# Joint score tiles, one low-rank add, key copies on ScalarE, and seven-product down projections from batch 1 on

## The chip, the cores and the metric

The kernel runs on one core of one Trainium2 chip. The metric is the device time of one execution in microseconds (us). The engines are named as in the profile: PE is TensorE's matmul, PEld its weight load, DVE VectorE, ACT ScalarE, POOL GpSimd, SP the engine that issues most DMAs. Each engine works through its own instructions in the order of the program and waits for the others by semaphores; an instruction that waits holds up all that stand behind it on its engine.

## The reference: what is computed

Four batches, 8 heads, 768 positions, head dimension 64. Attention with a local window of 96 positions and 8 global keys, with a linear bias by distance and a slope per head, and after it a mixer: a low-rank sum over positions (rank 32) and a feed-forward layer 512 to 2048 to 512.

```python
scores = scale * q @ k.T
rel = pos[:, None] - pos[None, :]
keep = is_global | ((rel >= 0) & (rel < n_local))
dist = where(is_global & ~is_local, n_local, abs(rel))
slopes = 2.0 ** (-8.0 * (arange(H) + 1) / H)
a = softmax(where(keep, scores - slopes * dist, -1e9))
x = concat_heads(a @ v)                # (4, 768, 512)
u = x + ((x.T @ U) @ V).T              # over positions, rank 32
out = u + relu(u @ w_ch1) @ w_ch2
```

With 8 heads the slope of head h+1 is half that of head h.

## The kernel before

**Tiling.** The program order is written out by hand (`manual_schedule`). Attention goes by pairs of heads: pair i is batch i // 4 and heads 2(i % 4) and the next one, 16 pairs. A pair's scores are three chunks of 512, 512 and 384 columns (diagonal blocks of 128 and the blocks beside them, with the 8 global keys copied into the first columns of the key blocks `kA`). A chunk of one head is one PSUM bank of 512 fp32 columns. PSUM's eight banks are the tags `sc` (2), `ob` (1), `cps` (2) and `th` (3).

**Batch 0** (pairs 0 to 3) adds the bias on PE (L352, a matmul with `slI` and `rel16`), and ACT takes the exponential from PSUM chunk by chunk (`st_SE`, L379). Its low-rank sum is made on PE too.

**Batches 1 to 3** add the bias on DVE: `st_S` makes a chunk's scores for both heads (`scores`, L360 and L367), and `s_dve` (L392) does one step for each head, score times scale over slope plus the table `relcat`, into `sp`; `st_E` (L404) takes the exponential of a whole head, 1408 columns. `st_V` multiplies by the values into `ob` (L416, L420), DVE normalises (L425, L439) and POOL makes an fp16 copy (L440). The low-rank sum of a pair is `st_M1` (L449, copied by L453), `st_MT` (L466, copied by L467) and `st_M3` (L503), whose result DVE adds to `x_sb` in two halves (L508), the first from `sc`, the second from `ob`; POOL copies to fp16 (L512), and `st_X` (L492) transposes by DMA into `uT`. The keys of a later pair are transposed by DMA (`turn`) and copied by DVE (`st_K`, L335 and L336).

**Feed-forward** goes by groups of 256 positions: group (b, g), three to a batch. A group has 8 up units (L609: 8 matmuls of 256 columns each; ACT's relu, L614, writes `htr`). Its down part is one of two kinds. Plain (`mk_down`): 8 units of four 512-column matmuls (L639), and two DVE adds (L644). Seven products (`mk_product`, the groups in `WG`): x1 to x4 into the bank `cx` and y1 to y3 into `cy`, each 8 matmuls of 256 columns (L659) and a DVE add of 256 columns into `x_sb` (L664), from sums s1 to s4 of halves of `htr` and t1 to t4 of quarters of the weights (L540). Each s is made in two halves of 512 columns: the first after four up units, the second after eight. A product's first four matmuls read the first half, its last four the second. In most groups the order of products is x1, y1, y2, x2, y3, x3, x4, in the last x1, y1, x2, y2, x3, y3, x4. y2 reads s1, x2 s2, y3 s4, x3 s3.

**The loop** of i = 4 to 17 (L774) sets the order around the change. One iteration does the scores of pair i, the values and low-rank sum of pair i-1, and between these steps `fill` (L691) issues units: 11 an iteration from i = 9 on. `unit` (L697) alternates an up unit of the next group with a down unit of the present one, as long as there are both. The up units of a batch are queued in the middle of i = 9, 13 and 17 (`queue_ff`); what is left after i = 17 is drained at the end. After each unit `fill` issues one queued DVE sum (`jobs`); a product that needs a sum that is not issued yet issues the sums up to it (`need`). Steps of an iteration, with units between them: scores chunk 0, values of the first head, chunk 1, values of the second head, chunk 2, M1, first exponential, MT, key copy of the next pair, M3, second exponential, transpose.

The weight sums t1, t2 and t4 (eight sums of 1024 columns with t3) are queued while the last plain group's down units run: group (2,0), in i = 14 and 15. Their tile takes one of the three `x_sb` buffers.

Of the kernel before, what the change touches and what calls it, by code (L numbers as in the profile page):

```python
# [20 lines left out]
def kernel(  # L21
# [17 lines left out]
    P = 128  # L39
# [28 lines left out]
    WG = ((2, 1), (2, 2), (3, 0), (3, 1), (3, 2))  # L68
# [11 lines left out]
    def ps_sc(tag="sc"):  # L80
        return psum.tile([P, 512], FP32, name="sc", tag=tag, bufs=2)
# [84 lines left out]
    setup = scp.tile([P, 384], I32, name="setup", tag="ep0")  # L166
# [16 lines left out]
    relcat = cst.tile([P, 640], FP32, name="relcat")  # L183
# [17 lines left out]
    for vt in vbuf:  # L201
        nc.gpsimd.memset(vt[:, :, :, D:D + 1], 1.0)
    nc.gpsimd.tensor_copy(relcat[:, 0:512].rearrange("p (a c) -> p a c", a=2), rel3[:, 0:2])
    nc.gpsimd.tensor_copy(relcat[:, 512:640], relB[:, 0:P])
    finish_table(
        relcat, relcat[0:NG, 0:512].rearrange("p (a c) -> p a c", a=2)[:, :, P:]
    )
# [22 lines left out]
    def new_batch(b):  # L230
        xs[b] = xp.tile([P, NSB, DM], FP32, name="x_sb", tag="x_sb", bufs=3)
        x16s[b] = xp.tile([P, NP, NSB, P], FP16, name="x16", tag="x16")
        tmps[b] = xp.tile([P, DM], FP16, name="tmp16", tag="tmp16", bufs=3)
        uTs[b] = xp.tile([P, NDC, S], FP16, name="uT", tag="uT")
# [97 lines left out]
    def st_K(i):  # L332
        kT = kts[i]
        kA = kp.tile([P, NSB - 1, P], FP16, name="kA", tag="kA")
        nc.vector.tensor_copy(kA.rearrange("d n p -> d (n p)"), kT[:, 0:S - P])  # L335
        nc.vector.tensor_copy(  # L336
            kA[:, 1:, 0:NG], kT[:, 0:NG].unsqueeze(1).broadcast_to((P, NSB - 2, NG))
# [5 lines left out]
    def scores(i, c, on_pe):  # L343
# [5 lines left out]
        scs = [ps_sc("cps" if on_pe and (i + c) % 2 else "sc") for hi in range(2)]  # L349
# [21 lines left out]
        return [(sc, c0, tot, r0) for sc in scs]  # L371

    def st_SE(i, c):

        if c == 0:
            for hi in range(2):
                eps[i, hi] = scp.tile([P, W], FP16, name=f"ep{hi}", tag=f"ep{hi}")
        for hi, (sc, c0, tot, _) in enumerate(scores(i, c, True)):
            nc.scalar.activation(  # L379
                eps[i, hi][:, c0:c0 + tot], sc[:, 0:tot], AF.Exp, scale=qk_scale  # L380
            )

    relfs = (relcat[:, 0:512], relcat[:, 256:512].unsqueeze(1).broadcast_to((P, 2, 256)), relcat[:, 256:640])

    def s_dve(i, hi, got):
        sc, c0, tot, r0 = got
        if c0 == 0:
            sps[i, hi] = scp.tile([P, W], FP32, name=f"sp{hi}", tag=f"sp{hi}", bufs=1)
        dst, got = sps[i, hi][:, c0:c0 + tot], sc[:, 0:tot]
        if c0 == 512:  # L390
            dst, got = (t.rearrange("p (a c) -> p a c", a=2) for t in (dst, got))
        nc.vector.scalar_tensor_tensor(  # L392
            out=dst, in0=got,
            scalar=qk_scale / slope[2 * (i % NP) + hi], in1=relfs[c0 // 512],
# [3 lines left out]
    def st_S(i, c):  # L398
        for hi, got in enumerate(scores(i, c, False)):
            s_dve(i, hi, got)  # L400

    def st_E(i, hi):
        ep = scp.tile([P, W], FP16, name=f"ep{hi}", tag=f"ep{hi}")
        nc.scalar.activation(  # L404
            ep, sps.pop((i, hi)), AF.Exp, scale=slope[2 * (i % NP) + hi]
        )
        eps[i, hi] = ep

    def st_V(i, hi):
        b, h = i // NP, 2 * (i % NP) + hi  # L410
        ep, vt, vA = eps.pop((i, hi)), vts[i], vas[i]
# [15 lines left out]
        x16 = x16s[b][:, i % NP, :, hi * D:(hi + 1) * D]  # L427
# [15 lines left out]
    def st_M1(i):  # L443
        b, dc = i // NP, i % NP
        ch = slice(dc * P, (dc + 1) * P)
        if b:
            tps = ps_ob()
            for n in range(NSB):
                nc.tensor.matmul(  # L449
                    tps[:, 0:R], x16s[b][:, dc, n], u16[:, n, 0:R],  # L450
# [5 lines left out]
        for n in range(NSB):  # L456
            nc.tensor.matmul(
                tps[:, 0:P], u16[:, n], x16s[b][:, dc, n],
# [10 lines left out]
    def st_M2(i):  # L469
        b, dc = i // NP, i % NP  # L470
        ch = slice(dc * P, (dc + 1) * P)
        for g in range(2):
# [5 lines left out]
            for t in range(NTG):  # L478
                nc.tensor.matmul(
                    ups[:, t * P:(t + 1) * P], x16s[b][:, dc, NTG * g + t], ident16,  # L480
# [9 lines left out]
    def st_X(i):  # L490
# [3 lines left out]
            x16s[b][:, dc].rearrange("p n d -> p (n d)"),  # L494
        )

    def st_M3(i, g):
        b, dc = i // NP, i % NP
        ch = slice(dc * P, (dc + 1) * P)
        ups = ps_ob() if g else ps_sc()  # L500
        for t in range(NTG):
            n = NTG * g + t
            nc.tensor.matmul(  # L503
                ups[:, t * P:(t + 1) * P], v16w[:, n * P:(n + 1) * P], tmps[b][:, ch],
# [386 lines left out]
```

## Time and profile before

| | us |
|---|---|
| median of 3 runs (lowest, highest) | 233.54 (232.63, 234.28) |
| the profiled execution | 232.94 |
| its span | 231.0 |
| from the span's start to the loop's first bias steps of i = 5 | 40.1 |
| i = 9 to 15, from one iteration's first bias step to the next | 12.04, 12.23, 12.01, 12.02, 12.21, 11.86, 12.30 |
| drain: last product's start | 226.64 |

The granted TensorE clock is 1.00 in every stretch. The page gives shares of busy time over the whole span; since matmuls overlap in the pipeline, a row's length is not what a matmul costs in a stream: that is read from the starts of rows that follow each other. A row of the time line with xN merges N instructions of one line. What the number in brackets after a row says is how long the engine sat idle before it, and which instruction ended that.

Rows of the groups that the change touches (busy us, mean ns of one):

```profile
L392 DVE SCALAR_TENSOR_TENSOR sp<-sc,relcat 128x512 f32<-128x512 f32 x48 | 31.0, 685 | 6.6 <-PE sc L367 5.7 <-ACT ep L404 0.4
...
L392 DVE SCALAR_TENSOR_TENSOR sp<-sc,relcat 128x384 f32<-128x384 f32 x24 | 12.3, 552 | 8.9 <-PE sc L360 8.9
...
L508 DVE TENSOR_TENSOR x_sb<-sc,x_sb 128x384 f32<-128x384 f32 x12 | 6.7, 556 | 3.8 <-PE sc L503 3.7
...
L335 DVE COPY kA<-kT 128x640 f16<-128x640 f16 x8 | 2.5, 319 | 0.2 <-DMA kT<-k 0.2
```

### The profile page before, as it was taken

How to read it: one execution, taken by the hardware profiler on the slowest of the kernel's cores; microseconds unless marked ns; L12 is line 12 of the kernel's file. 1: busy time of each engine (PE TensorE's matmuls, PEld its weight loads, DVE VectorE, ACT ScalarE, POOL GpSimd, SP SyncE). 2: the span in 40 equal slices, each digit the busy share in tenths (PEclk: the TensorE clock that was granted, in tenths of full speed). 3: DMA queues.
4: the chain of work that ended last, by engine and by line, in shares of the span. 5: the costliest groups of instructions: out<-in, count | busy, mean ns of one | idle time of the engine just before them, and what ended most of it. 6: DMA issues, size and time to landing. Idle time of an engine off the chain costs nothing.

```text
span 231.0 us, 5678 instructions
## 1 busy us (share of the span) xinstructions
PE 223.2 (97%) x2324; PEld 161.8 (70%) x2324; DVE 152.7 (66%) x350; ACT 110.9 (48%) x167; POOL 80.5 (35%) x131
## 2 busy tenths in 40 slices
PE   7989999999999999999999999999999999999994
PEld 2455678788644457766666656866688888888883
DVE  3697797868677667566656675779895524444452
ACT  6776957685621313827363707473633334333320
POOL 6399728577444243433424051504120100000000
PEclk9999999999999999999999999999999999999999
DMA  6997998999999999897786955633131302011112
GB/s 183 321 280 201 280 203 188 261 259 175 213 210 244 209 315 216 220 182 188 157 226 134 258 140 145 148 100 79 32 81 48 79 3 91 1 48 45 45 48 91
DMA packets 86561, 36.66 MB, mean 159 GB/s; under 512 B 74152, under 2 KB 83592, under 8 KB 86536
## 3 DMA queue, kind: packets, MB, share of 16 engines
q1 hardware_dynamic: 81480, 32.01, 55.1%
q0 software_dynamic: 5056, 4.29, 12.3%
q8 instruction: 18, 0.29, 0.5%
q14 instruction: 7, 0.06, 0.1%
HBM read 27.46 MB, written 6.29 MB: 146 GB/s over the span
## 4 chain that ended last, share of the span: by engine, by line
PE 86%; POOL 3%; DMA 3%; ACT 3%; DVE 2%; issue 1%; SPq 1%; POOLq 0%
PE hps L609 35%; PE cps L639 22%; PE cx L659 8%; PE cy L659 5%; PE sc L360 4%; DMA vst<-in_v_dram 3%; PE ob L420 2%; PE ob L416 2%; PE sc L367 2%; ACT htr L614 1%; ACT ep L404 1%; PE tp L250 1%; PE sc L503 1%; PE ob L503 1%; SPq L105 1%
## 5 line engine op out<-in xcount | busy, mean ns | idle before, releaser
L614 ACT ACTIVATE htr<-hps 128x512 f16<-128x512 f32 x96 | 56.6, 598 | 85.0 <-PE hps L609 82.2
L609 PE MATMUL hps<-uT,w 128*128 128x256 f16 x756 | 96.2, 273 | 0.5 <-DVE uT L485 0.3
L609 PEld LDWEIGHTS <-w 128*128 128x128 f16 x756 | 70.5, 98 | 11.3 <-issue 0.4
L639 PE MATMUL cps<-w,htr 128*128 128x512 f16 x224 | 56.9, 379 | 0.0
L392 DVE SCALAR_TENSOR_TENSOR sp<-sc,relcat 128x512 f32<-128x512 f32 (+1 forms) x72 | 43.3, 641 | 15.5 <-PE sc L360 8.9
L404 ACT ACTIVATE ep<-sp 128x1408 f16<-128x1408 f32 x24 | 32.8, 1374 | 16.3 <-DVE sp L392 16.3
L512 POOL CAST x<-x_sb 128x768 f16<-128x768 f32 x12 | 10.3, 856 | 60.5 <-DVE x_sb L508 60.5
L639 PEld LDWEIGHTS <-htr 128*128 128x128 f16 x224 | 19.1, 97 | 16.6
L440 POOL CAST x<-x_sb 128x384 f16<-128x384 f32 x30 | 15.8, 525 | 26.8 <-DVE x_sb L439 26.7
L360 PEld LDWEIGHTS <-kT 64*128 64x128 f16 x192 | 8.2, 93 | 15.1 <-issue 13.5
L540 DVE TENSOR_TENSOR s<-htr 128x512 f16<-128x512 f16 x20 | 9.3, 464 | 12.7 <-ACT htr L614 12.7
L439 DVE TENSOR_TENSOR x_sb<-ob,rcp 128x384 f32<-128x384 f32 x30 | 16.7, 558 | 1.0
L659 PEld LDWEIGHTS <-s 128*128 128x128 f16 x160 | 15.5, 98 | 1.8
L360 PE MATMUL sc<-qT,kT 64*128 64x128 f16 x192 | 16.7, 221 | 0.0
L420 PE MATMUL ob<-v,ep 128*128 128x65 f16 x192 | 16.2, 193 | 0.0
L420 PEld LDWEIGHTS <-ep 128*128 128x128 f16 x192 | 13.8, 98 | 2.7 <-ACT ep L379 0.3
L664 DVE TENSOR_TENSOR x_sb<-cx,x_sb 128x256 f32<-128x256 f32 x20 | 8.5, 423 | 10.1 <-PE cx L659 10.0
L136 POOL CAST v<-vst 128x768 f16<-128x768 f32 x16 | 13.4, 839 | 4.5 <-DMA vst<-in_v_dram 4.5
L367 PE MATMUL sc<-qT,kA 64*128 64x128 f16 x160 | 14.1, 216 | 0.9 <-DVE kA L286 0.9
L379 ACT ACTIVATE ep<-sc 128x512 f16<-128x512 f32 (+1 forms) x24 | 12.0, 559 | 5.1 <-PE sc L367 4.8
L416 PE MATMUL ob<-vA,ep 128*128 128x65 f16 x160 | 14.3, 194 | 0.2 <-DVE vA L312 0.2
L659 PEld LDWEIGHTS <-htr 128*128 128x128 f16 x120 | 11.7, 98 | 1.3
(102 smaller groups left out, 269.4 us busy)
## 6 DMA issues: line engine op xcount, KB each, us to landing
qst<-in_q_dram SPq DMA_DIRECT2D x16, 384.0 KB, 4.2
kst<-in_k_dram SPq DMA_DIRECT2D x16, 384.0 KB, 4.9
vst<-in_v_dram SPq DMA_DIRECT2D x16, 384.0 KB, 3.4
out_dram<-x_sb SPq DMA_DIRECT2D x23, 256.0 KB, 2.3
w<-in_moe_w_ch_dram POOLq DMA_DIRECT2D x8, 512.0 KB, 8.9
vA<-v SPq DMA_DIRECT2D x8, 152.3 KB, 4.3
out_dram<-x_sb SPq DMA_DIRECT2D x2, 128.0 KB, 1.7
uT<-x SPq DMA_TRANSPOSE x12, 2.8
```

What stands on the lines that cost most here:

```text
L360: nc.tensor.matmul(scs[hi][:, o:o + P], kT[r, kb * P:(kb + 1) * P], qT[r, kb * P:(kb + 1) * P], start=(o == 0 and not on_pe), stop=(o + P ...
L367: nc.tensor.matmul(scs[hi][:, o + P:o + 2 * P], kA[r, kb], qT[r, (kb + 1) * P:(kb + 2) * P], start=False, stop=(o + 2 * P == tot),)
L392: nc.vector.scalar_tensor_tensor(out=dst, in0=got, scalar=qk_scale / slope[2 * (i % NP) + hi], in1=relfs[c0 // 512], op0=ALU.mult, op1=ALU ...
L404: nc.scalar.activation(ep, sps.pop((i, hi)), AF.Exp, scale=slope[2 * (i % NP) + hi])
L416: nc.tensor.matmul(ob[:, qi], ep[:, OF[qi - 1]:OF[qi - 1] + P], vA[:, qi - 1, hi], start=True, stop=False,)
L420: nc.tensor.matmul(ob[:, qi], ep[:, DG[qi]:DG[qi] + P], vt[:, qi, hi], start=(qi == 0), stop=True,)
L439: nc.vector.tensor_tensor(xo, ob[:, :, 0:D], rb, ALU.mult)
L440: nc.gpsimd.tensor_copy(x16, xo)
L609: nc.tensor.matmul(hps[:, k * FT:(k + 1) * FT], w1_16[:, dc, jt * P:(jt + 1) * P], uT[:, dc, ts], start=(dc == 0 and k == 0), stop=(dc == ...
L614: nc.scalar.activation(cell["htr"][:, 2 * jp:2 * jp + 2].rearrange("p j t -> p (j t)"), hps, AF.Relu)
L639: nc.tensor.matmul(cps, htr[:, jc, t * P:(t + 1) * P], w2_16[:, jc], start=(b > 0 and jc == 0), stop=(jc == NJC - 1),)
L659: nc.tensor.matmul(ps, cell[a][:, j], tw[w][:, j], start=(first and j == 0), stop=(done is not None and j == HJ - 1), skip_group_check=True,)
```

## The change

- `WG` is every group of batches 1 to 3, nine in place of five. Groups (1,0), (1,1), (1,2) and (2,0) change from plain to seven products. The weight sums move to i = 8 and 9, and their tile is its own.
- `ps_sc` is one tile of two banks, one buffer, in place of two tiles of one bank. Both heads' scores go into it; in batch 0 every second chunk goes to `cps` as before, and where it goes to `sc` one exponential of both heads replaces two.
- `s_dve` is one step for both heads: scale over the first head's slope, and a table `relcat2` of two copies, the second times 0.5 (`st_R`, one DVE step of 768 columns in pair 2 of batch 0). `st_E` uses the first head's slope for both. `sp` and `ep` are one tile for both heads.
- `st_M3` writes all six blocks into the two-bank tile at the place of the first half, with one DVE add of 768 columns.
- `st_K`: ACT copies the 120 columns of each of the five key blocks, DVE the 8 global ones of each.
- The s sums are issued two units later (`wait=2`), and s3 is written over a part of `htr` (a21) in place of a tile of its own.
- The fp16 tile `x16` goes by pairs with three buffers in place of by batches with two.

```diff
-    WG = ((2, 1), (2, 2), (3, 0), (3, 1), (3, 2))
+    WG = tuple((b, g) for b in range(1, B) for g in range(NFG))
...
-    def ps_sc(tag="sc"):
-        return psum.tile([P, 512], FP32, name="sc", tag=tag, bufs=2)
+    def ps_sc():
+        return psum.tile([P, 2, 512], FP32, name="sc", tag="sc", bufs=1)
...
-        nc.vector.tensor_copy(kA.rearrange("d n p -> d (n p)"), kT[:, 0:S - P])
+        nc.scalar.copy(kA[:, :, NG:], kT.rearrange("d (n p) -> d n p", n=NSB)[:, 0:NSB - 1, NG:])
         nc.vector.tensor_copy(
-            kA[:, 1:, 0:NG], kT[:, 0:NG].unsqueeze(1).broadcast_to((P, NSB - 2, NG))
+            kA[:, :, 0:NG], kT[:, 0:NG].unsqueeze(1).broadcast_to((P, NSB - 1, NG))
         )
...
-        scs = [ps_sc("cps" if on_pe and (i + c) % 2 else "sc") for hi in range(2)]
+        both = None if on_pe and (i + c) % 2 else ps_sc()
+        scs = [ps_cps("sc") if both is None else both[:, hi] for hi in range(2)]
...
+    def st_R():
+        nc.vector.tensor_scalar_mul(relcat2[:, 1], relcat, 0.5)
+
+    relfs = (relcat2[:, :, 0:512], relcat2[:, :, 256:768], relcat2[:, :, 256:640])
...
         nc.vector.scalar_tensor_tensor(
-            out=dst, in0=got,
-            scalar=qk_scale / slope[2 * (i % NP) + hi], in1=relfs[c0 // 512],
+            out=sps[i][:, :, c0:c0 + tot], in0=both[:, :, 0:tot],
+            scalar=qk_scale / slope[2 * (i % NP)], in1=relfs[c0 // 512],
             op0=ALU.mult, op1=ALU.add,
         )
...
-    def st_M3(i, g):
+    def st_M3(i):
...
-        ups = ps_ob() if g else ps_sc()
-        for t in range(NTG):
-            n = NTG * g + t
+        ups = ps_sc()
+        for n in range(NSB):
+            g, t = divmod(n, NTG)
...
-        dst = xs[b][:, NTG * g:NTG * (g + 1), ch]
+        dst = xs[b][:, :, ch].rearrange("p (g t) d -> p g t d", g=2)
         nc.vector.tensor_tensor(
-            dst, ups[:, 0:GT].rearrange("p (t d) -> p t d", t=NTG), dst, ALU.add
+            dst, ups[:, :, 0:GT].rearrange("p g (t d) -> p g t d", t=NTG), dst, ALU.add
         )
...
-        jobs.append(go)
+        jobs.append((count[0] + wait, go))
...
-        t = xp.tile([P, 3, HJ, HD], FP16, name="t16", tag="x_sb", bufs=3)
+        t = wbig.tile([P, 3, HJ, HD], FP16, name="t16")
...
-                queue_sum((name, b, g), k, cell[name][:, js], cell[a][:, js], cell[b_][:, js], op)
+                queue_sum((name, b, g), k, cell[name][:, js], cell[a][:, js], cell[b_][:, js], op, wait=2)
...
             unit()
-            if jobs:
-                jobs.popleft()()
+            count[0] += 1
+            if jobs and jobs[0][0] < count[0]:
+                jobs.popleft()[1]()
...
-    s_dve(NP, 0, first[0])
+    s_dve(NP, first)
     begin_up(0, (0, 1), ps_cps("hps"))
     st_M1(NP - 1)
-    s_dve(NP, 1, first[1])
...
         if i > NP:
-            st_M3(i - 1, 0)
+            st_M3(i - 1)
...
         if i > NP:
-            st_M3(i - 1, 1)
             st_X(i - 1)
```

## The prediction, made before the changed kernel was run

> **What bounds the kernel now.** I read the page's busy shares and chain first, then busy time by stretches cut at the loop's iterations, then the order of time in the last 10 us and in the densest stretch of DVE. The page:
>
> ```profile
> PE 223.2 (97%) x2324; PEld 161.8 (70%) x2324; DVE 152.7 (66%) x350; ACT 110.9 (48%) x167; POOL 80.5 (35%) x131
> ...
> PE 86%; POOL 3%; DMA 3%; ACT 3%; DVE 2%; issue 1%; SPq 1%; POOLq 0%
> ```
>
> TensorE (PE) is the chain. The columns of the next view are stretch, length, then busy us and instructions of PE, PEld, DVE, ACT, POOL, the granted clock, DMA share and GB/s:
>
> ```profile
> 144.74:156.60 11.86, 11.86 (x133) 8.77 (x131) 9.25 (x22) 7.15 (x10) 3.77 (x7) 1.00 0.49 120
> 156.60:168.90 12.30, 12.30 (x126) 8.71 (x125) 11.34 (x26) 5.58 (x8) 2.83 (x4) 1.00 0.26 73
> ...
> 181.00:221.00 40.00, 40.00 (x369) 35.85 (x367) 17.38 (x45) 14.62 (x25) 0.00 (x0) 1.00 0.14 46
> ```
>
> The first two are the loop's iterations i=14 and 15 (attention of one head pair beside 11 units of feed-forward); the third is the drain, feed-forward alone. PE is never idle, and in the second DVE is at 92%: seven-product sums and attention there meet on DVE. What one unit costs PE, and what a wait costs, is in the drain's end (start us, length, engine, line):
>
> ```profile
> 222.27 1.04 PE L659 MATMUL cy<-w,htr 128*128 128x256 f16 x8
> 222.58 0.42 DVE L664 TENSOR_TENSOR x_sb<-cx,x_sb 128x256 f32<-128x256 f32 x1
> 222.91 0.41 DVE L540 TENSOR_TENSOR s<-s,htr 128x512 f16<-128x512 f16 x1
> 223.15 1.04 PE L659 MATMUL cx<-t,s 128*128 128x256 f16 x8
> 223.35 0.42 DVE L664 TENSOR_TENSOR x_sb<-cy,x_sb 128x256 f32<-128x256 f32 x1
> 223.69 0.42 DVE L540 TENSOR_TENSOR s<-htr,s 128x512 f16<-128x512 f16 x1
> 224.02 1.04 PE L659 MATMUL cy<-t,s 128*128 128x256 f16 x8
> 224.22 0.43 DVE L664 TENSOR_TENSOR x_sb<-cx,x_sb 128x256 f32<-128x256 f32 x1
> 224.56 0.42 DVE L540 TENSOR_TENSOR s<-htr 128x512 f16<-128x512 f16 x1
> ```
>
> Products follow each other every 0.873 us (223.15 to 224.02). The add of a product starts 0.20 after the next product starts (224.02 to 224.22), the sum queued behind it 0.34 later, and takes 0.42. A sum that needs the sum before it starts 0.45 after that one (191.47 to 191.92). PE goes on 0.06 after DVE:
>
> ```profile
> 176.22 0.18 DVE L453 CAST zw<-ob 128x32 f16<-128x32 f32 x1
> ...
> 176.46 0.23 PE L466 MATMUL ob<-ident,zw 128*128 128x128 f16 x1 [0.23 <-DVE zw L453]
> ```
>
> **The change part by part.** The profiled execution took 232.94 us (span 231.0); the median of the three shown is 233.54, 0.6 above. The sum is made against 232.94.
>
> *Fewer products.* Four more groups, (1,0), (1,1), (1,2) and (2,0), lose 8 down units of four 128x512 matmuls (0.862: 103.83 to 104.69) and get 7 products (0.873). 32 x 0.862 - 28 x 0.873 = 27.6 - 24.4: **-3.2 us** of PE. The loop issues the same number of units per iteration, so the drain is four units shorter. That is the whole gain: PE is the chain.
>
> *DVE.* Two 512-column bias steps take 1.19 from start to start of the next work, two of 384 columns 0.93:
>
> ```profile
> 156.60 1.28 DVE L392 SCALAR_TENSOR_TENSOR sp<-sc,relcat 128x512 f32<-128x512 f32 x2
> 157.79 0.69 DVE L644 TENSOR_TENSOR x_sb<-cps,x_sb 128x512 f32<-128x512 f32 x1
> 158.39 1.29 DVE L540 TENSOR_TENSOR t<-w,t 128x1024 f16<-128x1024 f16 x2
> 159.59 0.19 DVE L425 RECIPROCAL rcp<-ob 128x6 f32<-128x6 f32 x1
> ```
>
> So 1.02 ns a column and 0.075 fixed; a joint step is 1.12 (768 columns 0.86). That frees 36 x 0.075 = 2.7 us, the joint low-rank add 12 x 0.075 = 0.9, the key copies 8 x 0.3 = 2.4 (0.32 and 0.17 become one small copy of 0.17). Four groups add 8 sums and 7 adds at 0.34 each against two adds at 0.60: 4 x (5.1 - 1.2) = 15.6. DVE: +9.6 us. None of what is freed shortens the chain by itself. What is added matters where PE waits for it.
>
> *Joint bias step.* Now the first head's step is over 0.60 before the second's (0.47 for 384 columns); joined, both are over at about the second's time, so the first exponential starts some 0.4 later. It is used five units, 4.3 us, later: 0; on the chain it would be 11 pairs x 0.4 = 4.4 (rival 3). "Perfetto Trace Analysis" of the Trainium skill (Optimizing Scalar/DVE Operations) says that grouping pays if the engine is saturated, and that where it isn't but makes other engines wait, breaking instructions up may let work finish sooner; DVE at 66% is the second case, so that rule speaks against the joint step, the 4.3 us for it.
>
> *Sums two units later (wait=2).* While units of the next group alternate with products this hides. At three places a group's products follow each other with no next group: (1,2), (2,2), (3,2). In DVE's order of the changed program the second halves of the sums then stand behind the adds of the products just made, and the fifth matmul of the product that uses them waits for it. Before, (2,2) still had next units between, and (3,2) had its sums a place earlier.
> - Tail, (3,2): order add y1, s1, s2, then product x2. After y1's end: 0.20 + 0.34 + 0.45 + 0.42 + 0.06 = 1.47; x2's first half covers 0.44: 1.03. Later add y2, s3, then x3: 0.20 + 0.34 + 0.42 + 0.06 = 1.02, less 0.44: 0.58. **+1.6.**
> - (2,2), i=17, nothing between y1, y2, x2, y3, x3: y2 waits for y1's add (same bank) 0.20 + 0.42 + 0.06 = 0.68; x2, y3 and x3 each for a sum behind the previous add, 0.58. **+2.4.**
> - (1,2), i=13, attention between: y2 0.68 less the 0.43 of scores: 0.25; x2 waits for its sum behind a 1.12 bias step and y2's add: 0.9; y3 0.58 less the 0.33 of a value product: 0.25; x3 0.15; x4 waits for x3's add behind the next bias step: 0.7. **+2.2**; between 0.3 (no queue) and 3.1 (five waits of about 0.6).
>
> *Weight sums now at i=8 and 9.* Eight of 0.60 with two bias steps, two adds, a low-rank add and two normalisations (0.7 each) are 10.5 us of DVE between the key copy (81.0) and the end of the second head's normalisation (90.1): 1.4 late. The POOL copy behind it, which M1 needs, is now over 0.85 before M1 (90.68, 91.53), so M1 is late by about 0.6, and by 0.7 with the wait's own time: **+0.7** (0 as in i=14 and 15, where the same eight run now and PE waits nowhere; 1.5 if two such links are late).
>
> *Low-rank link.* tmp's copy stands behind an add and a sum in i=11 and 16; now a single add there (104.89) holds M3 to 105.83 instead of 105.62, 0.2. **+0.3** (0 to 1).
>
> *Start.* The joint first bias step ends 0.3 later than the half that stood before tmp's copy (30.45); st_R, 768 columns, lies between 0.5 (the 768-column cast, 545 ns) and 0.95, in a stretch with DVE gaps of 0.5. **+0.5** (0 to 1.2).
>
> *At nothing:* key copies on ACT, 600 columns, 0.66 each by the 384- and 768-column copies (475, 804 ns): they push the second exponential by 0.7 and the next bias step by up to 0.4, with two to three units before PE needs that bank; the cover goes if DVE is late by more than 1 us, ends 0 to 8 x 0.4 = 3. One tile for both heads' scores: the next chunk needed both banks before too. x16 with three buffers, the table copy on POOL, the low-rank add one unit earlier with its POOL copy and transpose: earlier or unused; SP's order of loads moves by that one unit.
>
> Sum: -3.2 + 1.6 + 2.4 + 2.2 + 0.7 + 0.3 + 0.5 = +4.5: **237.4 us**, 1.7% over the median of 233.54 (from the median's level it would be 238.0; inside the range).
>
> **Rivals.**
> 1. *Only the plain waits count*: tail and (2,2), 4.0, as (1,2) is covered by attention and the rest by DVE's gaps. 232.94 - 3.2 + 4.0 = 233.7; with half of (1,2) 234.8. For it: i=14 and 15 carry DVE at 78 to 92% with PE full. Against: the bias step in DVE's queue ahead of y2's add.
> 2. *DVE becomes the bound of i=9 to 15*: now 7.6 to 9.3 us busy an iteration up to i=14, plus three groups in four iterations x 3.9 = 2.9, less 0.5 freed = 2.4: 10 to 11.7 of 12.0. If order is lost too (key copies on ACT), each of seven iterations is 0.5 longer: 237.4 + 3.5 = 240.9. Against: 11.34 of 12.30 now, without a PE gap.
> 3. *The joint step's 0.4 reaches PE* in all 11 pairs: 237.4 + 4.4 = 241.8. It decides only where the exponential is used within a unit of its end. Against: five units lie between.
> 4. *Faster*: loop iterations differ now (11.86 to 12.30 for the same PE work), so PE already waits in the loop where its busy share hides it. If the 6 us that DVE is freed of take that away, the seven iterations from 84.23 to 168.90 at 11.86 save 84.7 - 83.0 = 1.7; and if the new waits only take the place of those, the tail alone stays: 232.94 - 3.2 - 1.7 + 1.6 = 229.6. It decides if (1,2) and (2,2) together cost under 1.5 us. Against: nothing lies between (2,2)'s products.
>
> That the change doesn't take PE work away is excluded: the changed program has the four units fewer.
>
> **How the numbers follow.** Forecast (235.9 to 239) 0.52; rival 1 (231.2 to 235.9) 0.26; rival 2 (over 239) 0.10; rival 3 0.03; rival 4 (under 231.2) 0.09. About 1%, 2.3 us, is what a measurement can tell from no change, so faster 0.09, same 0.26, slower 0.65. Range 232.5 to 240.0: it leaves out rival 4, rival 1's fastest end and most of rivals 2 and 3, 2 in 10 together. The forecast's own is 235.9 to 239, from the bounds of (1,2), the weight sums and the start.
>
> **What would show it.** Right: in the last 10 us, PE gaps of about 1.0 before x2's fifth matmul and 0.6 before x3's, released by DVE's sums; four gaps of 0.6 ahead of the drain; DVE near 162 us; the drain from its first up unit four units shorter. Wrong: products 0.873 apart in the tail; gaps in every iteration (rival 2); iterations all near 11.9 (rival 3).

## The result, and the profile after

| | before | after |
|---|---|---|
| median of 4 runs each (lowest, highest), us | 233.91 (232.63, 238.06) | 239.88 (239.79, 240.30) |
| the profiled execution, us | 232.94 | 239.79 |
| its span, us | 231.0 | 238.0 |

The ratio is 1.027, with a 95% interval of 1.023 to 1.031: slower, by about 6 us. Some executions, like that of 238.06 of the kernel before, are in a slower state; they stay in the medians and ranges here and below and are left out of the ratios. The forecast was 237.4, from 235.9 to 239, and the kernel is slower than that. The sum was made against the profiled execution, and there it stands at +4.5 forecast and +6.85 measured (+7.0 in the span).

The changed kernel's page, busy shares and the chain that ended last:

```profile
PE 223.2 (94%) x2420; PEld 170.1 (71%) x2420; DVE 164.7 (69%) x347; ACT 114.6 (48%) x169; POOL 84.3 (35%) x130
...
PE 65%; DVE 15%; POOL 6%; issue 4%; DMA 4%; ACT 2%; SPq 1%; DVEq 0%; POOLq 0%
```

PE is still the busiest engine, but its share has gone from 97% to 94%, and DVE's share of the chain from 2% to 15%. The engine totals don't tell where. Busy time by stretches does (stretch, length, then PE, PEld, DVE, ACT, POOL, clock, DMA share, GB/s); the stretches are i=9, 13 and 14, cut at the first score matmul of each iteration, and 40 us of the drain:

```profile
85.03:98.86 13.83, 12.74 (x133) 8.57 (x132) 11.97 (x21) 5.40 (x8) 5.83 (x7) 1.00 1.01 245
135.47:150.24 14.77, 12.98 (x148) 10.01 (x147) 10.77 (x22) 4.89 (x8) 4.55 (x7) 1.00 0.70 150
150.24:162.86 12.62, 12.32 (x147) 10.09 (x147) 10.73 (x23) 7.86 (x12) 4.55 (x7) 1.00 0.47 94
187.00:227.00 40.00, 38.28 (x346) 33.61 (x346) 17.10 (x44) 13.75 (x24) 0.00 (x0) 1.00 0.13 43
```

PE now misses 1.1 us in i=9, 1.8 in i=13, 0.3 in i=14 and 1.7 in the drain, where before it missed nothing in i=14, 15 and the drain. The difference of the two time lines, stretch by stretch (from first score matmul to first score matmul; MT is here the last transposing matmul of the low-rank sum, in i=16):

| stretch | before | after | difference | forecast of it |
|---|---|---|---|---|
| start to i=5 | 39.62 | 40.16 | +0.54 | +0.5 |
| i=5 and 6 | 20.63 | 21.56 | +0.93 | 0 |
| i=7 and 8 | 23.27 | 23.31 | +0.04 | 0 |
| i=9 | 12.25 | 13.83 | +1.58 | +0.7 |
| i=10 to 12 | 36.26 | 36.61 | +0.35 | +0.3 (with i=16) |
| i=13 | 11.99 | 14.77 | +2.78 | +2.2 |
| i=14 | 12.04 | 12.62 | +0.58 | 0 |
| i=15 to the last MT | 20.40 | 19.78 | -0.62 | 0 |
| MT to the last product's start | 50.18 | 51.02 | +0.84 | +0.8 (-3.2 + 1.6 + 2.4) |

The tail came as written. The changed kernel's time line near its end (start us, length, engine, line; in brackets the idle time before and who ended it):

```profile
228.54 0.60 PE L667 MATMUL cx<-t,s 128*128 128x256 f16 x4
...
229.53 0.43 DVE L548 TENSOR_TENSOR s<-s,htr 128x512 f16<-128x512 f16 x1
230.01 0.61 PE L667 MATMUL cx<-t,s 128*128 128x256 f16 x4 [0.87 <-DVE s L548]
```

x2's two halves stand 230.01 - 228.54 = 1.47 apart instead of 0.44: a gap of 1.03; x3's (231.33 and 232.34) leave one of 0.57. Forecast were 1.03 and 0.58. Both gaps end on a DVE sum that stands behind the add of the product before.

The four gaps of (2,2) are there too: y2 waits 0.52 by the trace's count for y1's add, x2, y3 and x3 each 0.41 for a sum (by starts: 0.68 and three times 0.58).

The misses are in the loop. The two largest kinds are these. One is the two-bank tile (i=5; the same in i=6):

```profile
50.28 0.96 DVE L515 TENSOR_TENSOR x_sb<-sc,x_sb 128x768 f32<-128x768 f32 x1 [0.99 <-PE sc L510]
51.29 0.23 PE L360 MATMUL sc<-qT,kT 64*128 64x128 f16 x2 [0.24 <-DVE x_sb L515]
```

M3's six blocks fill the tile, DVE empties it in one add of 0.96, and the next iteration's first scores need the same tile. In i=5 and 6 one unit lies between M3 and these scores, and it is over before the add is.

The other is DVE's queue in i=9:

```profile
93.13 0.56 DVE L446 TENSOR_TENSOR x_sb<-ob,rcp 128x384 f32<-128x384 f32 x1
...
93.61 0.68 DVE L548 TENSOR_TENSOR w<-w 128x1024 f16<-128x1024 f16 x1
93.76 0.90 POOL L447 CAST x<-x_sb 128x384 f16<-128x384 f32 x1 [1.94 <-DVE x_sb L446]
...
94.71 0.32 PE L456 MATMUL ob<-u,x 128*128 128x32 f16 x6 [0.83 <-POOL x L447]
```

From 82.8 to 95.2 DVE works without a gap. The second head's normalisation ends at 93.7, behind seven weight sums, adds and two bias steps. One of these sums, at 85.74, takes 1.29 instead of 0.68, beside two POOL copies. The POOL copy that reads the normalised values takes 0.90 instead of the 0.51 of other iterations; and PE, which has only M1 to go on with, stands idle for 0.83 until 94.71.

### The profile page after: what moved, and what is told of

It is laid out like the page before. It is cut to its first block, busy times and chain, and to the rows that moved or that the text cites. A ratio compares the mean times of both kernels' runs of the same rounds, so it can differ in the third digit from the quotient of the medians.

```text
span 238.0 us, 5850 instructions
## 1 busy us (share of the span) xinstructions
PE 223.2 (94%) x2420; PEld 170.1 (71%) x2420; DVE 164.7 (69%) x347; ACT 114.6 (48%) x169; POOL 84.3 (35%) x130
## 4 chain that ended last, share of the span: by engine, by line
PE 65%; DVE 15%; POOL 6%; issue 4%; DMA 4%; ACT 2%; SPq 1%; DVEq 0%; POOLq 0%
PE hps L617 27%; PE cx L667 11%; PE cy L667 8%; PE cps L647 7%; DVE sp L398 4%; DMA vst<-in_v_dram 3%; DVE x_sb L672 3%; PE sc L360 2%; DVE x_sb L446 2%; PE sc L510 2%; PE ob L427 2%; DVE s L548 1%; PE ob L423 1%; DVE t L548 1%; POOL x L447 1%
## 5 line engine op out<-in xcount | busy, mean ns | idle before, releaser
L398 DVE SCALAR_TENSOR_TENSOR sp<-sc,relcat 128x1024 f32<-128x1024 f32 (+1 forms) x36 | 40.7, 1130 | 8.7 <-PE sc L360 4.6
L667 PEld LDWEIGHTS <-htr 128*128 128x128 f16 x288 | 26.9, 98 | 5.8 <-DVE htr L548 1.7
L672 DVE TENSOR_TENSOR x_sb<-cx,x_sb 128x256 f32<-128x256 f32 x36 | 15.2, 422 | 21.7 <-PE cx L667 21.6
L447 POOL CAST x<-x_sb 128x384 f16<-128x384 f32 x30 | 16.7, 555 | 35.9 <-DVE x_sb L446 32.4
L667 PEld LDWEIGHTS <-s 128*128 128x128 f16 x216 | 20.1, 98 | 7.7 <-DVE s L548 4.4
L647 PE MATMUL cps<-w,htr 128*128 128x512 f16 x96 | 23.8, 379 | 0.0
L667 PE MATMUL cx<-w,htr 128*128 128x256 f16 x144 | 19.2, 273 | 0.9 <-DVE htr L548 0.8
L672 DVE TENSOR_TENSOR x_sb<-cy,x_sb 128x256 f32<-128x256 f32 x27 | 11.4, 422 | 11.8 <-PE cy L667 11.5
L515 DVE TENSOR_TENSOR x_sb<-sc,x_sb 128x768 f32<-128x768 f32 x12 | 11.5, 956 | 6.2 <-PE sc L510 6.2
```

The lines of the kernel that those rows point to most:

```text
L398: nc.vector.scalar_tensor_tensor(out=sps[i][:, :, c0:c0 + tot], in0=both[:, :, 0:tot], scalar=qk_scale / slope[2 * (i % NP)], in1=relfs[c0 ...
L447: nc.gpsimd.tensor_copy(x16, xo)
L647: nc.tensor.matmul(cps, htr[:, jc, t * P:(t + 1) * P], w2_16[:, jc], start=(b > 0 and jc == 0), stop=(jc == NJC - 1),)
L667: nc.tensor.matmul(ps, cell[a][:, j], tw[w][:, j], start=(first and j == 0), stop=(done is not None and j == HJ - 1), skip_group_check=True,)
L672: nc.vector.tensor_tensor(x_sb[:, n, cs], ps, x_sb[:, n, cs], ALU.add)
```

## The experiments

The kernel before has medians from 233.9 to 235.6 us in the comparisons below, so kernels that were not compared directly are set side by side by stretches of their traces. "Loop" is from the first score matmul of i=5 to the last MT (136.8 before, 142.5 after), "drain" from that MT to the end of the last matmul (51.2 and 52.1). In the edits, the new lines are those of each experiment against the changed kernel, if nothing else is said.

The theory to begin with, A, was the one of the forecast with the sizes corrected: sums that are issued two units late make PE wait. Its rival B: what costs is the DVE work of the added groups beside attention, with or without the delay.

### Which part of the change

**e1: no delay.**

```diff
-                queue_sum(..., op, wait=2)
+                queue_sum(..., op, wait=0)
```

> The changed kernel with the s sums issued at once again (wait=0), all else kept. If PE waits at the group ends because the sums stand behind the adds (theory A), the two gaps of the tail (1.0 and 0.6) and most of the four of (2,2) and the five of (1,2) go: 239.9 - 1.6 - 1.8 - 2 = 234.5, and products follow each other every 0.873 in the tail. If DVE's load in the loop is what costs (theory B), only the tail is better: 238.3.

Measured 241.44 (240.78 to 242.24), ratio to before 1.027 [1.020, 1.035]. Theory A fell, and B's 238.3 was missed too: without the delay the kernel is not faster at all. The drain is 48.5, 3.5 shorter, and in its tail products follow each other every 0.87 without a gap; but the loop is 147.5, 5.0 longer. 0.7 of that is i=7, ahead of the first sum of a product: a weight load came late there. What DVE waited for between 83 and 175 us of this kernel (us, times, longest) says why:

```profile
DVE s L548 <- ACT htr L622: 11.2, 9, 2.0
```

A sum issued right after its up unit waits for ScalarE's relu of that unit, up to 2.0 us when exponentials and key copies are ahead of it, and bias steps, adds and copies stand behind it. With two units of delay that row is absent. So the delay is worth about 4.3 in the loop and costs 3.5 from (2,2) on.

**e2: the five old groups**, all else as changed.

```diff
-    WG = tuple((b, g) for b in range(1, B) for g in range(NFG))
+    WG = ((2, 1), (2, 2), (3, 0), (3, 1), (3, 2))
```

> The changed kernel with the five seven-product groups of before, all else kept (wait=2 too). Theory A: the four units come back (+3.2), what (1,2), i=9 to 12 and i=14 cost goes (2.8, 1.9, 0.6), tail and (2,2) stay: 239.9 + 3.2 - 5.3 = 237.8. Theory B (the four new groups' load is the whole cost): near 234, as before the change.

Measured 236.62 (236.15 to 239.79), ratio 1.011 [1.008, 1.014]. Between the two. Loop 137.9, drain 52.8. So in the loop the four added groups, with the weight sums that move with them, cost 142.5 - 137.9 = 4.6, and all other edits 1.1: 0.9 of it in i=5 and 6, 0.2 in i=9. Its i=10 to 14 are as long as before to 0.01, with the joint bias steps, the key copies on ACT and the delay in them. The drain's 1.6 over before are the tail's.

**e3: M3 in halves**, first into one bank of the score tile, then into `ob`, an add of 384 columns each, as before the change.

```diff
-    def st_M3(i):
+    def st_M3(i, g):
...
-        ups = ps_sc()
+        ups = ps_ob() if g else ps_sc()[:, 0]
```

> The changed kernel with the low-rank sum's last step in two halves again, at the places and with the tiles (first bank of the score tile, ob) of before. In the trace of the changed kernel the scores of i=6 and 7 wait for the joint add, 0.3 to 0.6 an iteration; so 239.9 - 0.9 = 239.0 if that is all. If the joint add also holds later iterations (i=10 to 14), 238. If the add is hidden, 239.9.

Measured 239.47 (238.83 to 241.36), ratio 1.020 [1.011, 1.029]; the median is 0.4 lower, within its spread. The trace is clearer: i=5 and 6 take 10.8 and 10.1 instead of 11.1 and 10.4, i=9 0.3 less, and the loop 141.7 instead of 142.5; i=14 is 0.3 longer. In i=5:

```profile
50.22 0.56 DVE L515 TENSOR_TENSOR x_sb<-sc,x_sb 128x384 f32<-128x384 f32 x1 [0.82 <-PE sc L510]
...
51.08 0.23 PE L360 MATMUL sc<-qT,kT 64*128 64x128 f16 x2
```

The first half's add is over at 50.78, and the scores find the tile free. That is 0.6 of the 0.93 of i=5 and 6. The other 0.3 is M1 of i=5, which waits 0.12 to 0.13 (0.30 by starts) for a POOL copy in every run with the joint bias step, and not in the kernel before or in e4. By the rows it comes from the tile that the joint step writes for both heads: the first step in i=5 waits 1.23 for the exponential that reads this tile and starts 1.62 after the first scores, as the second head's step does before (1.61), where the first head's starts after 0.50.

**e4: the kernel before with the nine groups.** Needed for room: weight sums in a tile of their own, s3 over a21, `x16` by pairs, as in the change. No delay, separate bias steps, M3 in halves, key copies on DVE. The edit is against the kernel before.

```diff
-    WG = ((2, 1), (2, 2), (3, 0), (3, 1), (3, 2))
+    WG = tuple((b, g) for b in range(1, B) for g in range(NFG))
```

> The kernel before with nine groups by seven products (and with what makes room for it: the weight sums' tile of its own, s3 in place, x16 by pairs); bias steps by heads, M3 in halves, key copies on DVE and sums issued at once as before. Theory A: the four units saved (3.2) stand against the weight sums at i=8 and 9 (about 1.6) only: 233.5 - 3.2 + 1.6 = 232. Theory B: DVE has 9 us more than the changed kernel's relief leaves, and it is slower than the changed kernel or as slow: 239 or more.

Measured 239.21 (238.62 to 244.33), ratio 1.016 [1.004, 1.027]. B's number: the groups alone slow the kernel down. The loop is 145.2, 8.4 longer than before, of which about 1.5 are loads that came late in i=7 of this execution, so 6.9; the drain is 2.1 shorter (49.1). So the other edits of the change are the smaller part of what makes it slow (1.1 in the loop and 1.6 in the tail, by e2), and with them the nine groups cost less in the loop than without. No run takes the joint bias step or the key copies on ACT out alone.

### The delay by place

**f1: two units of delay in the loop, none from (2,2) on.** If e1 is read rightly, the gain of the one and the price of the other can be had apart.

```diff
-                queue_sum(..., op, wait=2)
+                queue_sum(..., op, wait=2 if (b, g) < (2, 2) else 0)
```

> The changed kernel, but the sums of the groups from (2,2) on are issued at once, as before the change; the earlier groups keep the two units of delay. Theory A: the delay pays in the loop, where without it DVE stood 11.2 us waiting for ScalarE's relu (i=9 to 17), and costs only from the start of the drain on, where from M's last transpose to the end PE took 52.1 us with the delay and 48.5 without. So the loop stays as in the changed kernel and the drain is 3.6 us shorter: 236.3. Rival B: the delay is not what the drain's time hangs on; what is saved there appears as DVE waits for the relu ahead of the products, and the time stays above 238.5.

Measured 236.93 (236.33 to 237.13), ratio 1.011 [1.008, 1.014]. A: every iteration is as long as in the changed kernel, and the drain is 48.5. Its end:

```profile
227.05 1.04 PE L667 MATMUL cx<-t,s 128*128 128x256 f16 x8
```

x2 is a single row of eight matmuls with no wait, and y2 starts 0.88 after it, at 227.93; x3 is such a row too. Both gaps of the tail are gone. One wait is left in the drain: y2 of (2,2), 0.67 for y1's add.

### The weight sums

**f2: six of the eight weight sums two groups earlier**, in i=7 and 8.

```diff
-                if (t, part) == (0, 1) and not split and follow in WG:
+                if (t, part) == (0, 1) and (b, g) == (0, 0):
```

> The changed kernel, but the six first weight sums are queued in group (0,0), two groups earlier, so they run in i=7 and 8 where DVE is busy 8 of 11.8 us, and only the two last ones stay in i=9. Theory A: i=9 is 1.6 us longer than i=11 because DVE works through a queue of 12 us without a gap there, and M1 waits 1.1 for the copy behind it. With 3 us taken out of that stretch the wait goes: 239.9 - 1.3 = 238.6. Rival B: DVE is the bound of all iterations from 9 on and the 3.6 us only move: i=8 gets longer by what i=9 loses, 239.9.

Measured 240.16 (239.57 to 242.5), ratio 1.028 [1.020, 1.037]. By the time, B. But the trace does not show DVE short of time. i=9 goes from 13.8 to 12.3, as A has it, and i=7 from 11.8 to 13.1, through one wait:

```profile
69.62 0.94 DVE L398 SCALAR_TENSOR_TENSOR sp<-sc,relcat 128x768 f32<-128x768 f32 x1
...
70.69 0.67 DVE L548 TENSOR_TENSOR t<-w,t 128x1024 f16<-128x1024 f16 x1
71.30 0.17 DVE L460 CAST zw<-ob 128x32 f16<-128x32 f32 x1
...
71.53 0.23 PE L473 MATMUL ob<-ident,zw 128*128 128x128 f16 x1 [1.12 <-DVE zw L460]
```

M1 is done at 69.5. The copy `zw` that MT needs takes 0.17 us, and it stands behind a bias step, a small copy of the values and a weight sum, until 71.3. One unit of PE, 0.9, lies between M1 and MT; the rest is the wait.

**f3: batch 1 plain**, the five old groups and (2,0); the weight sums fall into i=13.

```diff
-    WG = tuple((b, g) for b in range(1, B) for g in range(NFG))
+    WG = tuple((b, g) for b in range(2, B) for g in range(NFG))
```

> The changed kernel with seven products in batches 2 and 3 only (six groups: the five old ones and (2,0)); batch 1 is plain, the weight sums fall in (1,2). Theory A: a group whose products alternate with the next group's units costs PE nothing beside its own slots, so (2,0) gives its 0.8 us back: 236.6 with the five old groups becomes 235.8, and what the changed kernel lost lies in batch 1 (weight sums beside batch 1's attention, and (1,2) back to back). Rival B: every seven-product group beside attention costs about 1 us in the loop, (4.5 for four): 237.0.

Measured 238.39 (237.94 to 238.97), ratio 1.018 [1.015, 1.021]. Neither: slower than both expected, 1.8 over e2, all of it in the loop (139.7), where 0.5 is a weight load that came late in i=7. The drain is only 0.2 shorter than e2's, for in (2,2) y2 now waits 0.52. The same link is hit again: i=13 takes 13.2 instead of 12.0, and MT waits 0.91 in it for `zw`, which stands behind the last bias step and a weight sum. In e2 eight weight sums stood beside the same attention in i=14 and 15, and i=14 took 12.0: there the first of them happened to be issued after `zw`, not ahead of it. They were not free in i=15, though: its second head's values wait 0.26 for the first head's normalisation, and from MT to MT it takes 12.6 instead of 12.0.

**g1: f2, and no weight sum in the five units ahead of MT.** `quiet` is true from the second scores up to MT's copy; a weight sum is not issued while it is.

```diff
-            if jobs and jobs[0][0] < count[0]:
+            if jobs and jobs[0][0] < count[0] and not (quiet[0] and jobs[0][2]):
```

> The changed kernel with the weight sums queued in (0,0) as in the run before, and now issued only where no link of the low-rank chain is pending on DVE: not in the four units between the second scores' bias step and MT's copy. Moving them to i=7 alone had freed i=9 (13.8 to 12.3 us) and lengthened i=7 (11.8 to 13.1), where MT waited 1.12 for the small copy zw that stood behind two sums and a bias step in DVE's queue. Theory A (order): the sums cost through that place in the queue only; both iterations come down, 239.9 - 1.4 = 238.5. Rival B (capacity): DVE is short of time there, so the sums lengthen the iterations wherever they stand: 239.9 or more.

Measured 239.78 (239.12 to 240.40), ratio 1.025 [1.017, 1.032]: no gain. MT waits no longer, but the sums now stand ahead of M3's joint add:

```profile
72.83 0.68 DVE L549 TENSOR_TENSOR t<-w 128x1024 f16<-128x1024 f16 x1
73.43 0.95 DVE L515 TENSOR_TENSOR x_sb<-sc,x_sb 128x768 f32<-128x768 f32 x1
...
74.44 0.23 PE L360 MATMUL sc<-qT,kT 64*128 64x128 f16 x2 [0.71 <-DVE x_sb L515]
```

Chunk 1 of the same scores waits another 0.40 for the bias step behind the next sum, and i=8 takes 12.4 instead of 11.5. So order decides, as A says, but with the joint tile no place was left without a link behind it. With M3 in halves there is one: in g4 below the same sums in the same places leave 11.7, 11.9 and 12.2 in i=7, 8 and 9, 35.9 together, against 37.1 in the changed kernel and 35.5 before.

### Group (1,2)

**g2: one unit of delay instead of two for (1,2).**

```diff
-                queue_sum(..., op, wait=2)
+                queue_sum(..., op, wait=1 if (b, g) == (1, 2) else 2)
```

> The changed kernel with a delay of one unit instead of two for the sums of group (1,2) alone. In i=13 its x2 waits 0.75 and y2 0.20 for sums that stand behind the bias step of the second scores (1.21). Theory A: one unit earlier the first pair of sums is ahead of that step, and i=13 goes from 14.8 to about 13.9: 239.0. Rival B: the sums then wait for ScalarE's relu, or only push the bias step and the adds back by as much: 239.9.

Measured 238.87 (238.62 to 239.86), ratio 1.020 [1.012, 1.028]. A: 1.0 less, and i=13 takes 13.7 instead of 14.8. (The profiled execution lost 1.0 in i=7, where a weight load came late.) First the place in the changed kernel, then the same in g2:

```profile
135.91 0.88 DVE L548 TENSOR_TENSOR s<-htr 128x512 f16<-128x512 f16 x1
...
136.71 1.21 DVE L398 SCALAR_TENSOR_TENSOR sp<-sc,relcat 128x1024 f32<-128x1024 f32 x1
...
136.85 0.61 PE L667 MATMUL cy<-t,s 128*128 128x256 f16 x4 [0.20 <-DVE s L548]
...
138.18 0.41 DVE L548 TENSOR_TENSOR s<-s,htr 128x512 f16<-128x512 f16 x1
138.64 0.61 PE L667 MATMUL cx<-t,s 128*128 128x256 f16 x4 [0.75 <-DVE s L548]
```

```profile
136.26 0.92 DVE L548 TENSOR_TENSOR s<-htr 128x512 f16<-128x512 f16 x1
...
137.44 0.70 DVE L548 TENSOR_TENSOR s<-s,htr 128x512 f16<-128x512 f16 x1
...
138.06 1.21 DVE L398 SCALAR_TENSOR_TENSOR sp<-sc,relcat 128x1024 f32<-128x1024 f32 x1
```

In the first, x2's second sum is behind the bias step of 1.21; in the second both sums are ahead of it, and x2 (from 138.44) runs through. What is left is y2's wait for y1's add, 0.54, and x4's for x3's, 0.81.

**g3: f1, and the products of (1,2) and (2,2) take the banks in turns.**

```diff
-            for made in (x1, y1, x2, y2, x3, y3, x4) if last else (x1, y1, y2, x2, y3, x3, x4):
+            for made in (x1, y1, x2, y2, x3, y3, x4) if g == NFG - 1 else (x1, y1, y2, x2, y3, x3, x4):
```

> The kernel with the delay by place (sums at once from (2,2) on; 236.9, the loop as in the changed kernel), and the products of (1,2) and (2,2) take the two banks in turns, x1 y1 x2 y2 x3 y3 x4, as (3,2) does. Theory A: with x1 y1 y2 x2 ..., y2 waits for y1's add in the same bank, 0.4 in i=13 and 0.7 in i=17; in turns the add has a product's time. Less 0.9: 236.0. Rival B: what waits is DVE's queue and not the bank, so another product waits in its place: 236.9.

Measured 235.25 (234.94 to 238.25), ratio 1.010 [1.004, 1.015]: by the medians 1.7 under f1, where 0.9 was expected, but the two ratios, each to the kernel before in its own comparison, lie within each other's intervals. The traces account for 1.0: i=13 14.4 instead of 14.8, drain 47.9 instead of 48.5. In (2,2) this is A: y2 waited for the bank, and no other product waits in its place. In (1,2) it is rather B: y2 and x4 no longer wait, but x2 waits 1.91 for its sum.

### All together

**f4: f1, f2 and e3 together.**

> The changed kernel with three edits together: sums at once from (2,2) on, weight sums queued in (0,0), the low-rank sum M3 in two halves as before the change. Theory A: the three losses are separate, 3.6 + 1.3 + 0.8 = 5.7: 234.2, level with the kernel before. Rival B: DVE is the bound of the loop and takes back all but the drain's share: 236.5 or more.

Measured 236.49 (236.16 to 236.76), ratio 1.010 [1.007, 1.012]. B's number, and not for B's reason: f2's part gave nothing, since it had only moved its wait (i=7 13.5, i=9 12.3); the drain is 49.1, 0.6 more than in f1, since y2 of (2,2) waits 1.26 for y1's add and not 0.67.

**g4: f4 with the weight sums kept off the chain (g1), (1,2) at one unit (g2), and the first joint bias step behind the copy that the last M1 of batch 0 needs.**

```diff
-    s_dve(NP, first)
     begin_up(0, (0, 1), ps_cps("hps"))
     st_M1(NP - 1)
+    s_dve(NP, first)
```

> The changed kernel with all of it: M3 in two halves, sums of the products delayed by two units up to (1,1) and in (2,0) and (2,1), by one in (1,2), at once from (2,2) on, weight sums in (0,0) and clear of the low-rank chain, and the first joint bias step behind the copy that the last M1 needs (the copy came 0.75 later than before the change). Theory A: 236.5 with three of these, less 1.3 for the place of the weight sums, 0.9 for (1,2) and 0.3 for the start: 234.0, level with the kernel before. Rival B: 236.

Measured 235.18 (233.72 to 235.66), ratio 1.002 [0.998, 1.007]. 4.7 of the 6 us are back by the medians, 2.5 of 2.7% by the ratios; loop 140.1, drain 49.1. The time lies between A's 234.0 and B's 236.

**h1: g4 with g3's turns. h2: the same with batch 1 plain**, weight sums from (1,1) on.

```diff
-    WG = tuple((b, g) for b in range(1, B) for g in range(NFG))
+    WG = tuple((b, g) for b in range(2, B) for g in range(NFG))
...
-                if (t, part) == (0, 1) and (b, g) == (0, 0):
+                if (t, part) == (0, 1) and (b, g) == (1, 1):
```

> All the repairs (235.2) and the products of (1,2) and (2,2) in turns over the two banks, which shortened the stretch from the last transpose of M to the end by 0.8 us and i=13 by 0.4 when it was tried on the changed loop. Theory A: both add up here, 234.1. Rival B: in i=13 DVE's queue is what is waited for, and with the sums already a unit earlier only the 0.8 is left or less: 234.5 to 235.

> The same repairs, with batch 1 plain: seven products in batches 2 and 3 only, (2,0) the one group more than before the change; weight sums from (1,1) on and clear of the low-rank chain. Theory A: what is left of the longer loop hangs on batch 1, above all (1,2) back to back (13.7 us in i=13, 12.0 before); (2,0) alternates with next units and gives its 0.8, the turns in (2,2) another 0.7, the start costs 0.3: 1.2 below the kernel before on the same chip, ratio 0.995, and 1 us below the nine groups. Rival B: each added group costs its gain on DVE: level with the kernel before and with the nine groups.

h1: 233.97 (233.04 to 235.28), ratio 1.000 [0.997, 1.002]. h2: 233.49 (232.85 to 238.03), ratio 0.999 [0.995, 1.002]. h1 came as A expected (though of the 0.8 that the expectation takes for the drain from g3, the traces show 0.7). h2 lies 0.5 below h1 where 1.0 was expected (in its profiled execution a transpose by DMA came late and cost i=9 0.7), and its interval holds both 0.995 and 1: that it is faster than the kernel before can't be told. In h1 the drain is 2.8 shorter than before (48.4 against 51.2), and in the same 40 us of it PE misses nothing:

```profile
187.00:227.00 40.00, 40.00 (x369) 35.85 (x367) 17.99 (x46) 14.33 (x24) 0.00 (x0) 1.00 0.12 43
```

Its loop is 140.4, 3.5 longer than before: 1.3 of that in i=13, 0.9 in i=14, 0.8 in i=8, the rest in smaller steps that no run separates. In h2, with one added group, the loop is 138.0 and the drain 50.3, 1.2 longer and 0.9 shorter. So the gain of fewer products arrives in the drain, and the loop spends it. By the stretches most of h1's loss hangs on batch 1: without it, in h2, i=10 to 13 are as long as before to 0.01, and what stays is 0.3 in i=5, 0.4 in i=14 and the late transpose, less 0.3 after i=14. By the times it stays open, as the 0.5 between h1 and h2 is no more than that transpose.

## Why the prediction was right and wrong

**What failed: the price of the loop's waits.** The sum stood 2.5 us under the measured change of the span (+4.5 against +7.0), and all of that lies ahead of the last MT. Three places were priced too low or at nothing: the joint tiles in i=5 and 6 (0 against 0.93), the weight sums (0.7 against 1.58), and (1,2) with i=14 (2.2 against 3.36). The path was right: PE behind DVE's queue. -0.62 that nobody forecast hid a part of it: without that luck the sum would have been 3.1 short.

**Right: the sign and the kind.** The four units fewer shorten the drain (2.7 less in f1 than before), and waits of PE behind DVE's queue cost more than that. The tail (1.6 forecast, 1.60 measured) and the stretch from MT on (+0.8, +0.84) came to the tenth: every row that this sum needed was in the drain of the trace before.

**The start (+0.5, +0.54) came out by other parts.** `tmp`'s copy behind the joint first bias step stands at 31.20 instead of 30.45 and costs 0.32, as forecast. `st_R` costs 0.46, but not in DVE's queue. It runs beside a POOL copy, which takes 1.36 instead of 0.89; the next POOL copy is late by that, and PE's transposes of the keys at 23.95 wait 0.26 for it (0.46 by starts):

```profile
21.76 1.36 POOL L123 CAST q<-qst 128x768 f16<-128x768 f32 x1
```

All 14 runs with `st_R` have this copy of 1.36 and this wait; the two without it have neither. That the total fits is luck: PE came 0.24 earlier to this place than in the trace before.

**Wrong: "One tile for both heads' scores: the next chunk needed both banks before too", at nothing.** That looked at the scores alone. M3's first half had used one `sc` bank for 0.56 us and its second half `ob`; the joint M3 holds both banks for 0.96, with one unit to cover it in i=5 and 6. Cost: 0.6 of the 0.93 there by e3, and with it the free place in DVE's order that g1 then lacked. The other 0.3 belongs to *Joint bias step*, priced at 0: that looked at when the first exponential starts, and not at the joint step's own start, for which both heads' exponentials must be through with the tile (e3, above).

The Trainium skill (Perfetto Trace Analysis, Optimizing Scalar/DVE Operations) says that where DVE isn't saturated but makes other engines wait, breaking instructions up may let work finish sooner. The prediction weighed that for the bias step, where 0.3 in i=5 is all that shows; e3's trace agrees with it at M3: two adds of 0.56 leave PE no wait where one of 0.96 did.

**Wrong in size: the weight sums, 0.7 against 1.58.** The link was the right one (normalisation, POOL copy, M1), and DVE's stretch took 10.9 us (82.8 to 93.7) for the 10.5 forecast. In that two errors nearly cancel: only seven of the eight sums stand ahead of the normalisation's end, 0.6 less, and one of them takes 0.61 longer, beside POOL's copies. The POOL copy at 93.76 took 0.39 more than the row of the trace before. So M1's part is 1.0 (1.88 from the unit before it, where the trace before has 0.89) and not 0.7, and a second link was overlooked: the values of the second head wait 0.24, 0.6 by starts up to the next scores, for the first head's normalisation, which frees `ob`, at 90.21. (M1 stands at 91.64 in the trace before, not at the 91.53 of the sum.) The forecast's lower end, 0 as in i=14 and 15, was a coincidence of order: the same sums cost nothing behind `zw` in e2's i=14, 0.6 at the `ob` link in its i=15, and 1.2 ahead of `zw` in f3's i=13.

**Wrong in size: (1,2), 2.2 against 2.78,** inside its bounds of 0.3 to 3.1. All five waits named are there, and by starts x2 (0.91 for 0.9), y3 (0.26 for 0.25), x3 (0.24 for 0.15) and x4 (0.68 for 0.7) come to a tenth. y2 waits twice: 0.25 for y1's add, as forecast, and 0.36 (0.20 idle, at 136.85) for its own sum, which takes 0.88 at 135.91 instead of 0.42, beside a POOL copy. **Costed at nothing: i=14, +0.58:** MT waits there for `zw`, 0.30 by the trace's count, behind an add and a sum, the link that was priced for i=11 and 16.

**Not forecast: -0.62** between i=15 and the last MT. It lies between the MTs of the last two iterations, 11.46 before and 10.82 after. 0.40 of it is the wait that the prediction shows at 176.46: there `zw` stood behind a sum that had itself waited 1.08 for ScalarE's relu. The prediction took from these rows what a wait costs, and not that the delay would end this one. In the changed kernel and in e2 that MT does not wait. The other 0.24 lies ahead of it, at the second head's values, and what ended it is not shown.

So in three places a time was taken from rows in which POOL and DVE did not meet: in i=9 (0.39 and 0.61, together as much as M1 is late), in (1,2) (0.36) and at the start (0.46). No run keeps POOL's copies apart from DVE's work, so that these waits would vanish then is argued from the rows and not tested.

**Rival 2** (DVE the bound, every iteration longer, 240.9) is nearer in time, and e4 looked like it. The stretches speak against it: with DVE busy for 9.9 to 10.8 of 12.2 us, i=10 to 12 lose 0.35 together, while three other iterations lose 4.9. DVE is busy 163.9 us in g4 and 164.7 in the changed kernel, and g4 gets 4.7 back with M3 in halves and another order of the same work. DVE's total was forecast at 162; eleven of the changed kernel's 512-column sums take 0.49 to 1.02 instead of 0.42, 3.4 us more together, which covers the surplus (the last section says beside what).

**"Sums two units later" as pure loss** was the reading that fell. The prediction priced what the delay costs at group ends and not what it saves; e1 and f1 give both: about 4.3 saved in the loop, 3.5 lost in the drain.

## What to carry to other kernels

Work added to an engine that has gaps is free only where nothing that the bound engine needs stands behind it: in this kernel weight sums cost an iteration nothing or 1.2 to 1.4 us, depending on whether a copy of 0.17 us stood ahead of them or behind them in the same queue. So follow each short link through the program order and don't compare busy shares. A delay of issue has a best value for each place: long where the queue behind a waiting instruction is full of others' work, none where only its own consumer waits. Before two buffers are joined into one, look at every user of both, not only at the user that the joining is for, and at the time when the later of the two comes free. A time taken from a row holds where the other engines do then what they did beside that row.

## What the runs showed of the hardware

POOL's and DVE's instructions lengthen each other when both work on SBUF. The POOL copy of 384 columns takes 0.51 us alone and 0.90 when it starts beside a DVE sum of 1024 fp16 columns (93.76, above); in i=9 POOL is busy 5.83 us against 4.18 before, with seven instructions in both. The other way, a DVE sum of 512 columns takes 0.41 to 0.43 alone and 0.88 or 0.92 when a POOL copy has started 0.2 before it (135.91 and 136.26, above). The bias step, one of whose inputs is in PSUM, takes 1.21 behind them too, with a POOL copy running.

The Trainium skill (SBUF — State Buffer, SBUF: two separate sides) says that DVE and GpSimd take turns on a shared pair of ports, an exclusive lock held for a whole instruction, where a DVE instruction has two SBUF inputs or runs in a two-port mode. The trace agrees in kind, and shows the size: the one that starts second is longer by what the first still has to run, less 0.13 to 0.15. The copy at 93.76 starts 0.53 before the sum at 93.61 ends and is 0.39 longer; the sum at 135.91 starts 0.61 before the POOL copy at 135.69 ends and is 0.46 longer. From i=8 on, 13 sums and 18 POOL copies of the changed kernel that start with 0.16 to 0.75 of the other left all fit this; three sums with less than 0.1 left are not longer.
